# Holding three batches' tail loads behind a DMA transpose, in a linear-attention and feed-forward kernel

## The chip, the core and the metric

The kernel runs on one core of one Trainium2 chip. The metric is the device time of one execution in microseconds (us): 259.6 us is the median of three runs of the kernel before the change (259.32 to 260.02). A profile of one execution shows what each engine did: TensorE (PE in the profile, with its weight loads as PEld), VectorE (DVE), ScalarE (ACT), GpSimd (POOL) and SyncE (SP). SP and POOL are used here mostly to issue DMAs; SP's go by the hardware queue q1, POOL's by the software queue q0.

## What is computed

```python
def phi(x):
    return np.where(x > 0, x, np.exp(x) - 1.0) + 1.0
q_p, k_p = phi(q), phi(k)                      # q, k, v: (8, 8, 576, 64)
kv = np.einsum('bhsd,bhse->bhde', k_p, v)
z = np.sum(k_p, axis=2)
num = np.einsum('bhsd,bhde->bhse', q_p, kv)
den = np.einsum('bhsd,bhd->bhs', q_p, z)[..., None] + 1e-06
attn = num / den
x = attn.transpose(0, 2, 1, 3).reshape(8 * 576, 512)
a, b = x @ w1, x @ w2                          # (512, 1024) each
out = (a * b @ w3) @ w_out                     # (1024, 1024), (1024, 512)
```

All inputs and the output are float32; the kernel computes the matrix products in bfloat16.

## The kernel before

The 576 positions of each batch are split into 512 "main" positions (four rows of 128) and a tail of 64. Main positions are loaded in two halves of four heads each, 512 KB a load. The tails come as small DMAs of 64 KB: one for each half of the heads, so four for the q and k tails of a batch and two for its v tail. The 64-position tails of two batches share one row of 128, and all eight tails are collected into a ninth feed-forward block (c = 8). Since w3 and w_out are multiplied together once (wf), the feed-forward part is one product with w1, one with w2, an elementwise product and one product with wf.

All steps are emitted in one order, written out by hand as a list of short codes (ORDER, L520 to L546). Each engine executes its own instructions strictly in that order. A code is a letter, a batch (or block) and a part; a trailing "+" picks another engine for the step (for a load: POOL's queue in place of SP's; for a copy: VectorE in place of ScalarE). The codes that matter here:

- L, M, N: load of one half of k, q or v of a batch (load_qkv). R: tail load (load_tail), R4.0 for the q and k tails of batch 4, R4.1 for its v tail. The tail buffers are a ring of three for q and k and a ring of three for v, so the tails of one batch wait until those of an earlier batch have been used.
- x and X (exp on ScalarE), y and Y (max and add on VectorE), z and Z (min on VectorE): the three phi steps of k (small letters) and q (capitals). Part 2, as in x4.2, y4.2 and z4.2, is the step for both tails of the batch at once.
- v: copy of v into a bfloat16 tile; v4.2 is its tail.
- T: DMA transpose of phi(q) of a batch (qt_load, SP). It reads the whole tile qj, with the tails in it, and writes qt.
- K: kv and z of a batch (kv_full): 18 matmuls into a PSUM tile, then two copies. It needs k and v of the batch, with tails.
- A: num / den for one row of 128 positions (nat): four matmuls with qt as weights, then three VectorE instructions which leave xn. A4.4 and the like are the tail rows. K and A use the same PSUM tile, and there is only one such tile, so each waits until the one before has been read.
- D: DMA transpose of xn (xt_load, SP). F: one of the eight column blocks of the feed-forward product of a block (f_unit), eight matmuls in two PSUM banks, a copy on ScalarE and a product on VectorE; there are four such banks. O: 128 rows of output (o_unit), copied to o_sb. S: store of 256 rows (o_store, SP). There are two o_sb buffers, so the copy of an O step waits for the store of the second S step before.

SP executes its DMAs in the order of the list, so a transpose that waits for its input holds back all loads and stores behind it. Around the change the order on SP's queue is: T2.0, L3.0, N3.1, L3.1, L4.0, N3.0, S0.1, T3.0, D2.0, S0.0, L4.1, N4.1, M4.0, M4.1, M6.1, D3.0. On POOL's queue it is: R4.1 (two DMAs), R4.0 (four), R6.0 (four), R6.1 (two), R7.0 (four), R7.1 (two), and nothing behind these.

TensorE's order in the same place: A2.1, O0.0, ..., O1.1, O1.0, K3, O1.3, A3.0, O1.2, A3.2, F2.6, A3.3, F2.3, F2.1, A3.1, F2.0, F2.7, F2.4, F2.2, F2.5, A3.4, O2.3, F3.7, A2.4, F3.6.

GATES (L547) is a list of pairs "step<other": a load named there waits until the other step's DMA has completed. It acts in loaded (L551), which every load passes through; the wait is put on the last DMA of the load step. Before the change the list is empty.

Of the kernel before, what the change touches and what calls it, by code (L numbers as in the profile page):

```python
# [20 lines left out]
def kernel(  # L21
# [223 lines left out]

    def qt_load(b, part):
        t, s = qt_tile(b), ph["qt", b]
        i = NB if part else 0
        nc.sync.dma_start(out=t[:, i:NB + 2], in_=s[:, i * P:(NB + 2) * P], transpose=True)
# [271 lines left out]
    M0.0+ Y0.0 C1 E0 M0.1 I0 X0.0 E3 X0.1 L0.0 Y0.1 Z0.0 Z0.1 C0 y0.0 w0+ R0.0 R0.1 x0.0 E4 x0.2  # L521
    I1 w3+ L0.1+ x0.1 a0.0+ E1 y0.2 a0.1+ N0.1+ u0.2+ N0.0+ z0.0 R1.1 v0.1 y0.1 w4+ u3.2+ E2 w1+
    z0.2 z0.1 v0.0+ u4.2 E5 L1.0+ E7 v0.2+ E6 K0 M1.0+ M1.1+ w2 A0.3 y1.0 x1.0 L1.1+ u1.2 A0.0
    w5 R1.0+ u2.2+ w6 A0.2 B3.0 P0.3 Y1.0 z1.0 u5.2 I2 B3.1 X1.0 A0.1 w7+ P0.0 X1.1 Y1.1 N1.0+
    N1.1+ Z1.0 u6.2+ x1.2 P0.2+ x1.1 y1.2 P0.1 u7.2 Z1.1 y1.1 z1.1 B1.0 a1.0+ B1.1 v1.0+ B2.0
    B2.1 F0.6 B0.0 v1.1+ z1.2 T1.1 T0.1 v1.2 F0.7 M2.1 a1.1 K1+ F0.2 A1.2 F0.3 A1.3 F0.4 B0.1
    A1.0 P1.2 F0.5 P1.3 L2.1 A1.1 P1.0+ X2.1 R2.0+ h0 h1 A0.4 P1.1+ Y2.1 h2 h3 R3.0+ M3.1 i0
    A1.4 M2.0 i1 x2.1 X3.1 Z2.1 F1.7 F1.6 x2.2 L2.0 y2.1 y2.2 Y2.0 x3.2 R3.1+ X2.0 O0.3 N2.1
    x2.0 z2.1 N2.0 y2.0 z2.2 Z2.0 F1.0 M3.0 R5.0+ y3.2 T2.0 v2.1 L3.0 Y3.1 R2.1+ F1.5 N3.1 v2.0+
    z2.0 L3.1 Z3.1 v2.2+ O0.2 F1.2 F1.1 Y3.0 y5.2 z3.2 K2 F1.4 A2.2 X3.0 F1.3 L4.0 A2.3 x3.0  # L530
    O0.1 Z3.0 A2.0 x3.1 N3.0 y3.0 O0.0 v3.1 S0.1 A2.1 y3.1 R5.1+ z3.0 z3.1 v3.0 v3.2 O1.1+ O1.0
# [6 lines left out]
    L6.0 z6.2 O3.1 A5.2 L6.1 O3.0 A5.1 D1.1 Y6.1 Z6.1 F4.2 A5.0 Y6.0 F4.5 y6.1 F4.7 v6.0+ x6.1
    L7.0 x6.0 M7.0 A5.3 D3.1 x7.0 z6.1 F4.0 v6.1+ v6.2 F4.6 A4.4 Z6.0 F4.1 S3.0 F4.4 D5.0 A5.4
    y6.0 z6.0 F4.3 M7.1 F5.7 x7.2 y7.0 Y7.0 z7.2 L7.1 N7.0 K6+ z7.0 F5.6 F5.0 y7.1 X7.1 X7.0  # L540
    Z7.0 F5.5 S3.1 F5.3 Y7.1 T6.0 R7.1+ Z7.1 A6.3 T7.0 F5.1 O4.2 A6.1 x7.1 O4.1 A6.2 N7.1 z7.1
    F5.4 A6.0 F5.2 v7.1 v7.2+ O4.0 D6.0 D5.1 A6.4 v7.0 O4.3+ S4.1 K7 O5.0 F6.3 S4.0 O5.1 A7.4
    F6.5 F6.4 D7.1 F6.1 A7.3 O5.2 O5.3 A7.1 F6.2 F8.3 A7.0 F8.6 S5.1 F6.6 A7.2 S5.0 F6.0 F6.7
# [120 lines left out]
```

## Time and profile before

| | |
|---|---|
| median of three runs | 259.6 us |
| span of the profiled execution | 257.4 us |
| moved by DMA | 50.57 MB, mean 196 GB/s |
| share of the 16 DMA engines: SP's queue q1, POOL's queue q0 | 55.9%, 23.4% |
| full qt transposes, from issue to landing | 4.6 to 11.1 us |
| xt transposes, median from issue to landing | 4.4 us |

The profiled execution has its own time, the span; the runs' times lie about 2.2 us above it. "Busy" is the time in which an engine executes something, and an idle time is put down to what released the engine in the end. Times within the execution are microseconds from the start of its span. In a row of the timeline the first number is the start and the second the duration; "x2" says that two instructions are merged, and the bracket at the end is the idle time before with its releaser. A DMA's duration on SP or POOL is that of its issue, not of its transfer; "us to landing" runs from the issue to the completion.

### The profile page before, as it was taken

To read this page: it belongs to the slowest core of one execution; us is meant where nothing else is said; L and a number is where in the kernel's file an instruction comes from. 1 tells how busy PE (TensorE), PEld (TensorE's weight loads), DVE (VectorE), ACT (ScalarE), POOL (GpSimd) and SP (SyncE) were. 2 spreads that over 40 slices of the span, in tenths; PEclk is the share of its full clock that TensorE was granted. 3 is DMA by queue.
4 is the path that set the end of the run, shared out by engine and by line. 5 is a ranking of instruction groups with operands and counts; after the bars stand their busy time and mean duration, and the time that the engine had idled before them with its cause. 6 is when DMAs were issued, how large, how long until landed. Compare 5 with 4: busy or idle time off the path is not lost.

```text
span 257.4 us, 3788 instructions
## 1 busy us (share of the span) xinstructions
PE 232.3 (90%) x1352; PEld 117.8 (46%) x1368; DVE 159.1 (62%) x350; ACT 116.8 (45%) x180; POOL 49.1 (19%) x84
## 2 busy tenths in 40 slices
PE   0087899999999869999999999999999999999992
PEld 0063565554454434445445445454544444444540
DVE  0548589778899426897887899978235633343200
ACT  1404677357756506755562473645332312332221
POOL 8524479455045100600000000000000000000000
PEclk9999999999999979999999999999999999999999
DMA  6999999999989999799999998646512143001124
GB/s 220 211 237 289 311 255 245 200 248 283 299 247 291 194 242 347 182 284 222 356 308 211 289 263 272 154 89 151 200 20 91 74 83 163 3 0 30 42 115 139
DMA packets 63762, 50.57 MB, mean 196 GB/s; under 512 B 33536, under 2 KB 58368, under 8 KB 63744
## 3 DMA queue, kind: packets, MB, share of 16 engines
q1 hardware_dynamic: 54432, 37.10, 55.9%
q0 software_dynamic: 9152, 13.11, 23.4%
q8 instruction: 10, 0.16, 0.3%
q10 hardware_dynamic: 160, 0.13, 0.2%
q14 instruction: 8, 0.07, 0.1%
HBM read 38.80 MB, written 9.44 MB: 187 GB/s over the span
## 4 chain that ended last, share of the span: by engine, by line
PE 78%; DMA 13%; DVE 4%; issue 2%; ACT 0%; POOL 0%; DVEq 0%; ACTq 0%; POOLq 0%
PE a_ps L322 24%; PE b_ps L322 23%; PE o_ps L479 21%; DMA v<-in_v_dram 5%; DMA qt<-qj 4%; PE nd L280 4%; DMA wt_sb<-in_moe_w_out_dram 4%; PE kvp L225 2%; PE wf_ps L143 1%; PE kvp L229 1%; DVE y L173 1%; DVE vt L204 1%; PE o_ps L504 1%; DVE kj L198 1%; DVE qj L198 0%
## 5 line engine op out<-in xcount | busy, mean ns | idle before, releaser
L322 PEld LDWEIGHTS <-w_sb 128*128 128x128 bf16 x576 | 55.3, 98 | 61.8 <-issue 0.9
L328 DVE TENSOR_TENSOR ab<-a_sb,b_ps 128x512 bf16<-128x512 f32 x72 | 49.1, 685 | 38.2 <-PE b_ps L322 30.5
L322 PE MATMUL a_ps<-xt,w_sb 128*128 128x512 bf16 x256 | 67.3, 382 | 0.0
L322 PE MATMUL b_ps<-xt,w_sb 128*128 128x512 bf16 x256 | 66.7, 379 | 0.0
L327 ACT COPY a_sb<-a_ps 128x512 f32<-128x512 f32 x72 | 41.8, 585 | 54.4 <-PE a_ps L322 48.9
L479 PE MATMUL o_ps<-wf_sb,ab 128*128 128x512 bf16 x267 | 63.7, 383 | 0.8 <-issue 0.2
L479 PEld LDWEIGHTS <-ab 128*128 128x128 bf16 x280 | 27.0, 98 | 30.2 <-issue 0.8
L481 ACT COPY o_sb<-o_ps 128x512 f32<-128x512 f32 x29 | 16.8, 585 | 43.4 <-PE o_ps L479 27.2
L286 DVE TENSOR_TENSOR xn<-nd,r 128x512 bf16<-128x512 f32 x32 | 22.1, 691 | 1.1
L168 ACT ACTIVATE e<-q 128x1024 bf16<-128x1024 f32 x16 | 16.7, 1056 | 8.5 <-DMA q<-in_q_dram 8.5
L168 ACT ACTIVATE e<-k 128x1024 bf16<-128x1024 f32 x16 | 16.6, 1056 | 5.2 <-DMA k<-in_k_dram 5.0
L280 PE MATMUL nd<-kv,qt 128*128 128x130 bf16 (+1 forms) x160 | 16.1, 223 | 2.6 <-DMA qt<-qj 2.1
L136 PE MATMUL w3p<-ident,w3b 128*128 128x128 bf16 x64 | 5.7, 242 | 13.7 <-DMA w3b<-in_moe_w_dram 13.7
L280 PEld LDWEIGHTS <-qt 128*128 128x128 bf16 (+1 forms) x160 | 11.6, 101 | 14.0 <-issue 3.3
L284 DVE TENSOR_SCALAR r<-nd 128x8 f32<-128x8 f32 (+1 forms) x40 | 6.5, 162 | 16.8 <-PE nd L280 16.4
L173 DVE TENSOR_SCALAR y<-q 128x1024 bf16<-128x1024 f32 x16 | 11.2, 707 | 8.7 <-DMA q<-in_q_dram 8.7
L143 PE MATMUL wf_ps<-wt_sb,w3t 128*128 128x512 bf16 x61 | 14.9, 380 | 0.7 <-DMA wt_sb<-in_moe_w_out_dram 0.5
L104 POOL DMA_DIRECT2D qk32r<-in_q_dram x14 | 9.0, 648 | 19.1 <-ACT a_sb L327 16.5
L198 DVE TENSOR_TENSOR qj<-e,y 128x512 bf16<-128x512 bf16 x32 | 11.9, 417 | 0.4 <-ACT e L168 0.3
L198 DVE TENSOR_TENSOR kj<-e,y 128x512 bf16<-128x512 bf16 x32 | 11.9, 418 | 0.2
L225 PE MATMUL kvp<-vt,kj 128*128 128x130 bf16 x128 | 9.8, 219 | 2.4 <-DVE vt L204 1.8
L136 PEld LDWEIGHTS <-w3b 128*128 128x128 bf16 x64 | 4.6, 109 | 15.0 <-DMA w3b<-in_moe_w_dram 14.5
(54 smaller groups left out, 180.3 us busy)
## 6 DMA issues: line engine op xcount, KB each, us to landing
out_dram<-o_sb SPq DMA_DIRECT2D x16, 512.0 KB, 3.7
q<-in_q_dram SPq DMA_DIRECT2D x13, 512.0 KB, 8.0
k<-in_k_dram SPq DMA_DIRECT2D x13, 512.0 KB, 6.7
v<-in_v_dram SPq DMA_DIRECT2D x12, 512.0 KB, 8.0
w3b<-in_moe_w_dram POOLq DMA_DIRECT2D x8, 256.0 KB, 12.0
v<-in_v_dram POOLq DMA_DIRECT2D x4, 512.0 KB, 9.8
w_sb<-in_moe_w_dram POOLq DMA_DIRECT2D x8, 256.0 KB, 6.9
q<-in_q_dram POOLq DMA_DIRECT2D x3, 512.0 KB, 11.2
```

What stands on the lines that cost most here:

```text
L143: nc.tensor.matmul(wfs[i], w3ts[i][:, kc, :], wo_sb[:, kc, :], start=(kc == 0), stop=(kc == FC - 1))
L168: nc.scalar.activation(out=e, in_=x, func=AF.Exp)
L173: (nc.gpsimd if alt else nc.vector).tensor_scalar(out=y, in0=x, scalar1=0.0, scalar2=1.0, op0=ALU.max, op1=ALU.add)
L198: nc.vector.tensor_tensor(out=p[0][:, 2 * g + c].rearrange("p j u d -> p u j d"), in0=e[:, c], in1=y[:, c], op=ALU.min)
L225: nc.tensor.matmul(kvp[:, i, g * W:(g + 1) * W], kj[:, hp, j].rearrange("p u d -> p (u d)"), vt[:, j, 2 * hp:2 * hp + 2, :].rearrange("p h ...
L280: nc.tensor.matmul(nd[rows, g, i * 2 * E1:(i + 1) * 2 * E1], w, kvs[b % 2][:, i, g].rearrange("p u e -> p (u e)"), start=True, stop=True)
L286: nc.vector.tensor_tensor(out=dst.rearrange("p (g h) e -> p g h e", g=2), in0=v4[:, :, :, 0:D], in1=r[rows].unsqueeze(3).to_broadcast([n, ...
L322: nc.tensor.matmul(ps, w[:, kc, f * P:(f + 1) * P], xt_of(c)[:, :, kc, :], start=(kc == 0), stop=(kc == KC - 1))
L327: nc.scalar.copy(out=a_sb, in_=a_ps)
L328: nc.vector.tensor_mul(out=abs_[c][:, f, :], in0=a_sb, in1=b_ps)
L479: nc.tensor.matmul(o_ps, ab[:, f, m * P:(m + 1) * P], wf_sb[:, f, :], start=(f == 0), stop=(f == FC - 1))
L481: copy_of(alt)(out=rows_of(c, m // 2)[:, m % 2], in_=o_ps)
```

## The change

One list of steps is replaced by another, one gate is added, and the T step records its DMA so that a gate can name it. The computation stays the same. In the list:

- L4.0 moves from a place ahead of A2.3 to one behind S0.0; on SP's queue it thereby goes from ahead of N3.0, S0.1, T3.0, D2.0 and S0.0 to behind them.
- v4.2+ moves from behind L4.1 to behind Z4.1.
- y4.2 and x4.2 move from around F2.7 to behind X4.0, and z4.2 from behind Z4.0 to ahead of it.
- The gate R4.1<T3.0 makes the second of R4.1's two DMAs on POOL's queue wait for the completion of T3.0. What stands behind it in that queue (R4.0, R6.0, R6.1, R7.0, R7.1) can't be issued earlier either.

Cut to the lines that differ in content:

```diff
-        nc.sync.dma_start(out=t[:, i:NB + 2], in_=s[:, i * P:(NB + 2) * P], transpose=True)
+        return nc.sync.dma_start(out=t[:, i:NB + 2], in_=s[:, i * P:(NB + 2) * P], transpose=True)
...
-    Y3.0 y5.2 z3.2 K2 F1.4 A2.2 X3.0 F1.3 L4.0 A2.3 x3.0
+    Y3.0 y5.2 z3.2 K2 F1.4 A2.2 X3.0 F1.3 A2.3 x3.0
...
-    T3.0 D2.0 S0.0 K3 R4.1+ R4.0+ O1.3 A3.0 O1.2 A3.2 L4.1 v4.2+ F2.6 A3.3 F2.3 N4.1 y4.1 F2.1
-    M4.0 x4.1 A3.1 x4.0 F2.0 M4.1 y4.2 M6.1 v5.2+ x4.2 F2.7 Y4.0 D3.0 F2.4 z4.1 X4.1 F2.2 Y4.1
-    v4.1 S1.0 F2.5 Z4.1 M5.0 N4.0 X4.0 Z4.0 A3.4 z4.2 y4.0 O2.3 F3.7 M5.1 Y5.0 v4.0 A2.4 F3.6
+    T3.0 D2.0 S0.0 L4.0 K3 R4.1+ R4.0+ O1.3 A3.0 O1.2 A3.2 L4.1 F2.6 A3.3 F2.3 N4.1 y4.1 F2.1
+    M4.0 x4.1 A3.1 x4.0 F2.0 M4.1 M6.1 v5.2+ F2.7 Y4.0 D3.0 F2.4 z4.1 X4.1 F2.2 Y4.1
+    v4.1 S1.0 F2.5 Z4.1 v4.2+ M5.0 N4.0 X4.0 y4.2 x4.2 z4.2 Z4.0 A3.4 y4.0 O2.3 F3.7 M5.1 Y5.0 v4.0 A2.4 F3.6
...
-    GATES = ""
+    GATES = "R4.1<T3.0"
...
         elif t == "T":
-            qt_load(b, i)
+            held[s] = qt_load(b, i)
```

More of the change, by code (lines that the diff above doesn't have):

```diff
@@ L520 @@
     ORDER = """
[L521 to L531, printed above, removed]
@@ L532 @@
-    T3.0 D2.0 S0.0 K3 R4.1+ R4.0+ O1.3 A3.0 O1.2 A3.2 L4.1 v4.2+ F2.6 A3.3 F2.3 N4.1 y4.1 F2.1
-    M4.0 x4.1 A3.1 x4.0 F2.0 M4.1 y4.2 M6.1 v5.2+ x4.2 F2.7 Y4.0 D3.0 F2.4 z4.1 X4.1 F2.2 Y4.1
-    v4.1 S1.0 F2.5 Z4.1 M5.0 N4.0 X4.0 Z4.0 A3.4 z4.2 y4.0 O2.3 F3.7 M5.1 Y5.0 v4.0 A2.4 F3.6
-    z4.0 L5.0 T4.0 R6.0+ x5.2 Y5.1 X5.0 F3.1 N5.1 Z5.0 S1.1 O2.2+ K4 F3.2 M6.0 x6.2 X5.1 A4.2
-    Z5.1 F3.4 z5.2 F3.5 y5.0 A4.1 F3.0 L5.1 F3.3 N5.0 y5.1 X6.1 y6.2 O2.1 A4.3 R6.1+ N6.0 S2.1
-    x5.1 N6.1 v5.0+ T5.0 O2.0 x5.0 v5.1+ A4.0 R7.0+ z5.1 D4.0 z5.0 X6.0 O3.3 y7.2 O3.2+ K5+ S2.0
@@ L538 @@
[L538 to L543, printed above, removed]
@@ L544 @@
-    D7.0 O6.3+ O6.2 O6.1 O6.0+ F7.1 F7.7 F7.2 F8.0 S6.1 F8.7 S6.0 F8.1 F8.5 F7.4 F8.2 F8.4 F7.6
-    O8.2 F7.5 H8.2 F7.3 F7.0 Q8.3 O7.0 O7.1 O7.2 S7.0 O7.3 O8.0 S7.1 O8.1 S8.0
+    M0.0+ Y0.0 C1 E0 M0.1 I0 X0.0 E3 X0.1 L0.0 Y0.1 Z0.0 Z0.1 C0 y0.0 w0+ R0.0 R0.1 x0.0 E4 x0.2 I1
+    w3+ L0.1+ x0.1 a0.0+ E1 y0.2 a0.1+ N0.1+ u0.2+ N0.0+ z0.0 R1.1 v0.1 y0.1 w4+ u3.2+ E2 w1+ z0.2
+    z0.1 v0.0+ u4.2 E5 L1.0+ E7 v0.2+ E6 K0 M1.0+ M1.1+ w2 A0.3 y1.0 x1.0 L1.1+ u1.2 A0.0 w5 R1.0+
+    u2.2+ w6 A0.2 B3.0 P0.3 Y1.0 z1.0 u5.2 I2 B3.1 X1.0 A0.1 w7+ P0.0 X1.1 Y1.1 N1.0+ N1.1+ Z1.0
@@ new lines @@
+    u6.2+ x1.2 P0.2+ x1.1 y1.2 P0.1 u7.2 Z1.1 y1.1 z1.1 B1.0 a1.0+ B1.1 v1.0+ B2.0 B2.1 F0.6 B0.0
+    v1.1+ z1.2 T1.1 T0.1 v1.2 F0.7 M2.1 a1.1 K1+ F0.2 A1.2 F0.3 A1.3 F0.4 B0.1 A1.0 P1.2 F0.5 P1.3
+    L2.1 A1.1 P1.0+ X2.1 R2.0+ h0 h1 A0.4 P1.1+ Y2.1 h2 h3 R3.0+ M3.1 i0 A1.4 M2.0 i1 x2.1 X3.1 Z2.1
+    F1.7 F1.6 x2.2 L2.0 y2.1 y2.2 Y2.0 x3.2 R3.1+ X2.0 O0.3 N2.1 x2.0 z2.1 N2.0 y2.0 z2.2 Z2.0 F1.0
+    M3.0 R5.0+ y3.2 T2.0 v2.1 L3.0 Y3.1 R2.1+ F1.5 N3.1 v2.0+ z2.0 L3.1 Z3.1 v2.2+ O0.2 F1.2 F1.1
@@ new lines @@
+    Y3.0 y5.2 z3.2 K2 F1.4 A2.2 X3.0 F1.3 A2.3 x3.0 O0.1 Z3.0 A2.0 x3.1 N3.0 y3.0 O0.0 v3.1 S0.1
+    A2.1 y3.1 R5.1+ z3.0 z3.1 v3.0 v3.2 O1.1+ O1.0 T3.0 D2.0 S0.0 L4.0 K3 R4.1+ R4.0+ O1.3 A3.0 O1.2
+    A3.2 L4.1 F2.6 A3.3 F2.3 N4.1 y4.1 F2.1 M4.0 x4.1 A3.1 x4.0 F2.0 M4.1 M6.1 v5.2+ F2.7 Y4.0 D3.0
+    F2.4 z4.1 X4.1 F2.2 Y4.1 v4.1 S1.0 F2.5 Z4.1 v4.2+ M5.0 N4.0 X4.0 y4.2 x4.2 z4.2 Z4.0 A3.4 y4.0
+    O2.3 F3.7 M5.1 Y5.0 v4.0 A2.4 F3.6 z4.0 L5.0 T4.0 R6.0+ x5.2 Y5.1 X5.0 F3.1 N5.1 Z5.0 S1.1 O2.2+
@@ new lines @@
+    K4 F3.2 M6.0 x6.2 X5.1 A4.2 Z5.1 F3.4 z5.2 F3.5 y5.0 A4.1 F3.0 L5.1 F3.3 N5.0 y5.1 X6.1 y6.2
+    O2.1 A4.3 R6.1+ N6.0 S2.1 x5.1 N6.1 v5.0+ T5.0 O2.0 x5.0 v5.1+ A4.0 R7.0+ z5.1 D4.0 z5.0 X6.0
+    O3.3 y7.2 O3.2+ K5+ S2.0 L6.0 z6.2 O3.1 A5.2 L6.1 O3.0 A5.1 D1.1 Y6.1 Z6.1 F4.2 A5.0 Y6.0 F4.5
+    y6.1 F4.7 v6.0+ x6.1 L7.0 x6.0 M7.0 A5.3 D3.1 x7.0 z6.1 F4.0 v6.1+ v6.2 F4.6 A4.4 Z6.0 F4.1 S3.0
+    F4.4 D5.0 A5.4 y6.0 z6.0 F4.3 M7.1 F5.7 x7.2 y7.0 Y7.0 z7.2 L7.1 N7.0 K6+ z7.0 F5.6 F5.0 y7.1
+    X7.1 X7.0 Z7.0 F5.5 S3.1 F5.3 Y7.1 T6.0 R7.1+ Z7.1 A6.3 T7.0 F5.1 O4.2 A6.1 x7.1 O4.1 A6.2 N7.1
@@ L546 @@
+    z7.1 F5.4 A6.0 F5.2 v7.1 v7.2+ O4.0 D6.0 D5.1 A6.4 v7.0 O4.3+ S4.1 K7 O5.0 F6.3 S4.0 O5.1 A7.4
+    F6.5 F6.4 D7.1 F6.1 A7.3 O5.2 O5.3 A7.1 F6.2 F8.3 A7.0 F8.6 S5.1 F6.6 A7.2 S5.0 F6.0 F6.7 D7.0
+    O6.3+ O6.2 O6.1 O6.0+ F7.1 F7.7 F7.2 F8.0 S6.1 F8.7 S6.0 F8.1 F8.5 F7.4 F8.2 F8.4 F7.6 O8.2 F7.5
+    H8.2 F7.3 F7.0 Q8.3 O7.0 O7.1 O7.2 S7.0 O7.3 O8.0 S7.1 O8.1 S8.0
     """
-    GATES = ""
+    GATES = "R4.1<T3.0"
     ctx.enter_context(tc.manual_schedule())
```

## The prediction

> **What bounds the kernel now.** I read the share of the engines and the 40 slices first, then the waits, then the timeline round the one hole that they show, then the DMA traffic in that hole.
>
> ```profile
> PE 232.3 (90%) x1352; PEld 117.8 (46%) x1368; DVE 159.1 (62%) x350; ACT 116.8 (45%) x180; POOL 49.1 (19%) x84
> PE   0087899999999869999999999999999999999992
> PEclk9999999999999979999999999999999999999999
> DMA  6999999999989999799999998646512143001124
> ```
> A slice is 6.4 us. TensorE is the bound from slice 8 on, but for slices 13 and 14 (84 to 97 us): there it is 80% and then 60% busy, and the only dip of its granted clock before the end lies there. The DMA engines are nearly full until 160 us, so traffic that is moved stays somewhere.
>
> ```profile
> PE nd L280 <- DMA qt<-qj: 2.1, 1, 2.1
> PE kvp L225 <- ACT vt L204: 0.6, 1, 0.6
> ACT vt L204 <- DMA v<-in_v_dram: 5.8, 4, 1.9
> ACT o_sb L481 <- DMA out_dram<-o_sb: 16.2, 3, 8.5
> ```
> The waits that cost TensorE time after 60 us: 2.1 us for a transposed q (step A3.0 waits for T3.0), and 0.6 us for a cast of v (K3 waits for v3.0, which waits for load N3.0).
>
> ```profile
> 90.20:92.20 2.00, 0.00 (x0) 0.00 (x0) 0.00 (x0) 0.00 (x0) 0.00 (x0) 1.00 1.18 192
> 92.20:93.20 1.00, 0.97 (x8) 0.62 (x9) 0.47 (x3) 0.00 (x0) 0.00 (x0) 1.00 1.49 134
> 93.20:96.60 3.40, 3.40 (x13) 1.47 (x12) 1.33 (x4) 0.00 (x0) 0.00 (x0) 0.50 1.08 304
> 96.60:100.00 3.40, 3.40 (x21) 1.60 (x19) 1.50 (x5) 2.05 (x4) 0.00 (x0) 0.99 1.10 345
> ```
> Busy time by stretch (PE, PEld, DVE, ACT, POOL), then granted clock, DMA share and GB/s. All engines stand still from 90.2 to 92.2 while DMA is full; one microsecond after TensorE starts again its clock is halved for 3.4 us, which costs 3.4 x (1 - 0.50) = 1.7 us.
>
> ```profile
> 74.22 1.23 POOL L104 DMA_DIRECT2D v32r<-in_v_dram  x2 [12.16 <-DVE vr L210]
> 75.09 1.25 SPq L489 DMA_DIRECT2D out_dram<-o_sb  x1
> 77.94 1.23 POOL L104 DMA_DIRECT2D qk32r<-in_q_dram  x2
> 81.07 5.93 SPq L249 DMA_TRANSPOSE qt<-qj  x1
> 82.02 0.77 POOL L104 DMA_DIRECT2D qk32r<-in_k_dram  x1 [0.65 <-DMA v32r<-in_v_dram]
> 87.09 3.89 SPq L311 DMA_TRANSPOSE xt<-xn  x1
> 91.07 0.62 SPq L489 DMA_DIRECT2D out_dram<-o_sb  x1
> ```
> Start, duration, engine. T3.0 goes out at 81.07 and lands 11.1 us later, at 92.17; D2.0 (87.09, lands after 8.3) and store S0.0 (91.07, after 6.6) queue behind it. Ahead of T3.0 on SP's queue stand five loads (L3.0, N3.1, L3.1, L4.0, N3.0, issued 72.1 to 75.0) and store S0.1. Beside them POOL issues R4.1, R4.0 and R6.0 from 74.22 to 82.8.
>
> ```profile
> DMA packets 1451, 1.45 MB, mean 362 GB/s; under 512 B 39, under 2 KB 1451, under 8 KB 1451
> q1 hardware_dynamic: 1451, 1.45, 105.1%
> DMA packets 1001, 1.17 MB, mean 259 GB/s; under 512 B 108, under 2 KB 919, under 8 KB 1001
> q1 hardware_dynamic: 828, 0.83, 79.2%
> q0 software_dynamic: 173, 0.34, 30.5%
> ```
> DMA in 74.5 to 78.5 us (two lines) and in 79.0 to 83.5 us (three). SP's queue (q1) moves 1.45 / 4.0 = 0.363 MB per us alone, and 0.83 / 4.5 = 0.184 beside the tails (q0).
>
> **The change, part by part.** No arithmetic is added or removed; every piece is a shift.
>
> *Ahead of T3.0.* L4.0 (0.524 MB) leaves the queue: 0.524 / 0.363 = 1.4 us. The second half of R4.1 and all of R4.0 and R6.0 (9 DMAs of 64 KB, 0.59 MB) wait: in 79.0 to 83.5 the tails cost q1 4.5 x (0.363 - 0.184) = 0.8 MB, or 2.2 us. The same q1 traffic then ends thus: L3.1 landed at 79.6 (73.3 + 6.3), before the first tail did (80.4), N3.0 now comes 1.4 us later, S0.1 another 1.4: about 82.5, not 87.2. So T3.0 meets an almost empty queue. Its own time is not shown for that place; the nearest rows bound it: 4.6 us (T7.0, the shortest of the full qt transposes) and 7.4 (T4.0, issued behind a full queue). It lands at 85.7 to 88.5; I take 86.5, nearer the free one.
>
> *What TensorE then does.* N3.0 lands near 81.1 instead of 85.7 (74.4 + 11.3), so ACT's second cast starts at 84.1, behind the first, instead of 85.73. K3 starts when O1.0 ends at 86.2 (kj is ready at 85.86): 0.6 us won. It lasts 1.4 us (86.83 to 88.24), O1.3 1.7 us: A3.0 can start at 89.3, against 92.23. Even the late bound 88.5 is hidden by K3 and O1.3. Without the hole of 2.1 us I expect no clock dip: 1.7 us. Together 0.6 + 2.1 + 1.7 = 4.4 us; bounds 2.7 (dip stays) and 4.7 (small gaps close too). [...] The stretch 93.2 to 96.6 comes right behind the hole, so I go by the row.
>
> *The next in line.* F2.6 (95.56 before, 91.5 then) needs D2.0. D2.0 now waits for A2.1's xn (83.91), moves behind T3.0's data and lands at 88.5 to 91.3: 4.4 us (D3.0, undisturbed) behind 84.1, or 8.3 less 1 behind 84.0. Hidden, by 0.2 us at the late end. S0.0 goes out near 87 instead of 91.07 and lands 3.7 us (median of the stores) to 6.6 us later, at 90.7 to 93.6; ACT's copies of O1.3 and O1.2 wait for it, and F2.1 (95.4) wants the bank that ACT's next copy frees, so 93.7 is the last good time. Hidden too, narrowly at the late end.
>
> *POOL.* Behind the gated DMA stand R4.0, R6.0, R6.1, R7.0 and R7.1 and nothing else. They start at about 86.5 and their data meets S0.0, L4.0, L4.1 and N4.1. [...] L4.1 is wanted by y4.1 at 101.55 - 4.4 = 97.1. Queue: D2.0 done 88.5, S0.0 1.4, then 1.05 MB at 0.184 = 5.7, landing 0.8: 96.4. I cost it at nothing, at most 0.5. L4.0 lands before it and is used after it.
>
> *The moved phi steps.* v4.2 (0.63 us of DVE from its start to the next), y4.2 (0.34) and z4.2 (0.34) now stand ahead of Z4.0 and A3.4 on DVE. Before, DVE waits 0.36 to 0.44 us for TensorE ahead of each of the products at 107.18, 108.91 and 110.64, so taking them away from earlier places wins nothing. A3.4's xnr ends at 113.82 before, 1.3 later now, and A2.4 on TensorE, at 114.36 with no wait, shares its PSUM tile: 113.82 + 1.31 - 114.36 = 0.8 us lost (bounds 0 and 1.3). x4.2 moves behind X4.0 on ACT, which has idle time there (1.5 us before 112.74). T4.0 is issued at the same place, as its last input ends at about 114.0 against 114.28. R7.0 must now wait for y4.2.
>
> Sum: -4.4 + 0.8 = -3.6 us. Span 257.4 to 253.8. The profiled span stands 2.2 us below the median of 259.6, so the time is 259.6 - 3.6 = 256.0 us. From 97 us on TensorE has no wait over 0.2 us, so nothing later swallows the gain.
>
> **Rivals.**
> (1) The dip has another cause and stays: 259.6 - 2.7 + 0.8 = 257.7. For it: TensorE is busy again for a whole microsecond before the clock falls. [...] Against: it is the one dip before the end, behind the one hole of that size since 60 us.
> (2) T4.0 takes T3.0's place. Before, it lands at 121.75 and A4.2 runs at 122.75: slack 1.0. R7's six tails now start about 3 us later in the program and may fall beside T4.0 as R6.0's did beside T3.0. If T4.0 too takes 11.1 from 114.0 - 4.4 = 109.6, it lands at 120.7, A4.2 wants it at 122.75 - 3.6 = 119.1: 1.6, and 1.7 if the clock falls: 256.0 + 3.3 = 259.3. Half of that, or a late L4.1, gives 257 to 258. Against: only 0.4 MB of tails, and one load less than ahead of T3.0.
> (3) Slower: the released tails hold S0.0 at its old landing, 97.7. Then ACT frees F2.6's bank at 97.7 + 1.07 + 0.6 = 99.4, and F2.1 waits from 95.4: 4.0, with a new dip 5.7: 256.0 + 5.7 = 261.7. It decides from a landing of 93.7, and is slower than before from 95.6 on with the dip. For it: S0.0 stands behind two transposes and beside nine tails. Against: SP is free for it 4 us sooner.
> (4) The change does not do it: T3.0 stays slow although the queue is empty (T5.0 took 11.1 with no tails beside it). Then A3.0 waits as before and only A2.4's 0.8 is new: 260.4. Against: T5.0 had eight DMAs ahead of it.
>
> **How the numbers follow.** Forecast 0.66 (255.2 to 256.8 by the terms' own bounds); rival 1 0.08; partial 2 at 257 to 258 0.09, full 2 0.05; rival 3 0.08; rival 4 0.04. A measurement of this kernel (259.32 to 260.02) tells about 0.3%, 0.8 us, from no change. Faster: 0.66 + 0.08 + 0.09, less a little for the edges, 0.82. Same: full 2 and edges, 0.07. Slower: 3, most of 4: 0.11. The range runs from 255.0 to 258.2, over forecast, rival 1 and partial 2, which leaves out about 0.2.
>
> **What would show it.** T3.0 lands 5 to 7 us after its issue; no TensorE wait at A3.0 and K3; granted clock 1.00 from 88 to 96; S0.0 landed before 93.7; a wait of A2.4's nd on DVE of about 0.8 us near 110. Wrong if TensorE shows a new wait over 1 us at F2.6, F2.1 or A4.2, or a second dip.

## The result, and the profile after

The changed kernel is slower: a median of 262.73 us against 259.38 (nine runs of each), ratio 1.0092 with a 95% interval of 1.0064 to 1.012. The profiled execution's span is 260.7 us against 257.4. The forecast was 256.0, with a range from 255.0 to 258.2. (Here and below the ratio is worked out over the undisturbed executions alone, the medians are of all, and the one isn't the quotient of the others.)

The share of the engines and the 40 slices of the changed kernel:

```profile
PE 233.0 (89%) x1352; PEld 117.7 (45%) x1368; DVE 159.3 (61%) x350; ACT 117.0 (45%) x180; POOL 49.3 (19%) x84
PE   0087999999999999785999999999999999999992
PEclk9999999999999999999799999999999999999999
DMA  6999999999999999999999989826701343000225
```

The weak slices 13 and 14 of before (84 to 97 us) are full now, and so is the clock there. New weak slices stand at 16 to 18 (104 to 124 us), and a dip of the clock right behind them. The stall at T3.0 is gone, and a longer one stands some 30 us later. The waits of the changed kernel from 60 to 130 us name it (total us, times, longest):

```profile
ACT e L168 <- DMA q<-in_q_dram: 4.1, 2, 2.3
PE nd L280 <- DMA qt<-qj: 3.9, 1, 3.9
PE nd L280 <- DVE xnr L286: 0.7, 1, 0.7
PE o_ps L479 <- DVE ab L328: 0.6, 1, 0.6
PE a_ps L322 <- DMA xt<-xn: 0.6, 1, 0.6
```

To see where time was won and lost, follow the same instructions in both traces. TensorE's timeline has, of the kernel before, the first matmuls of A3.4, A2.4, A4.2 and A4.1 (start, duration):

```profile
110.46 0.41 PE L280 MATMUL nd<-kv,qt 128*64 128x130 bf16 x4
114.36 0.41 PE L280 MATMUL nd<-kv,qt 128*64 128x130 bf16 x4
122.75 0.39 PE L280 MATMUL nd<-kv,qt 128*128 128x130 bf16 x4
126.43 0.39 PE L280 MATMUL nd<-kv,qt 128*128 128x130 bf16 x4
```

and of the changed kernel A3.4, O2.3, F3.7, A2.4 and A4.2, with the wait in front of each:

```profile
105.62 0.41 PE L280 MATMUL nd<-kv,qt 128*64 128x130 bf16 x4
...
108.00 0.82 PE L479 MATMUL o_ps<-wf_sb,ab 128*128 128x512 bf16 x3 [0.61 <-DVE ab L328]
...
109.40 1.04 PE L322 MATMUL a_ps<-xt,w_sb 128*128 128x512 bf16 x4 [0.57 <-DMA xt<-xn]
...
112.02 0.41 PE L280 MATMUL nd<-kv,qt 128*64 128x130 bf16 x4 [0.72 <-DVE xnr L286]
...
124.47 0.61 PE L280 MATMUL nd<-kv,qt 128*128 128x130 bf16 x4 [3.89 <-DMA qt<-qj]
```

At A3.4 the changed kernel leads by 110.46 - 105.62 = 4.84 us. At A2.4 the lead is 114.36 - 112.02 = 2.34: three waits (0.61, 0.57, 0.72) and small gaps took 2.5. At A4.2 it is 122.75 - 124.47 = -1.72: another 4.06 lost, of which 3.89 is one wait for T4.0, the DMA transpose of batch 4's q. A4.1 starts at 129.73 against 126.43, so 1.58 more went by there; from then on the changed kernel is 3.30 behind to the end. The windows show what that last piece is (PE, PEld, DVE, ACT, POOL, then granted clock, DMA share, GB/s):

```profile
122.00:124.30 2.30, 0.00 (x0) 0.00 (x0) 0.00 (x0) 0.00 (x0) 0.00 (x0) 1.00 1.12 223
124.30:127.70 3.40, 3.23 (x11) 1.47 (x12) 1.73 (x5) 0.59 (x1) 0.00 (x0) 0.50 1.07 336
127.70:131.00 3.30, 3.30 (x19) 1.60 (x18) 2.02 (x4) 0.59 (x1) 0.00 (x0) 1.00 1.10 356
```

The same pattern as before the change, at another transpose: all engines still, DMA full, then a clock of 0.50 for 3.4 us. The timeline of SP's and POOL's queues of the changed kernel shows what stood beside the transposes (start, duration of the issue):

```profile
81.26 2.82 SPq L249 DMA_TRANSPOSE qt<-qj  x1
84.17 3.16 SPq L311 DMA_TRANSPOSE xt<-xn  x1
88.25 0.62 POOL L104 DMA_DIRECT2D v32r<-in_v_dram  x1 [13.21 <-DMA qt<-qj]
...
99.05 6.36 SPq L311 DMA_TRANSPOSE xt<-xn  x1
110.15 1.23 POOL L104 DMA_DIRECT2D qk32r<-in_q_dram  x2 [12.01 <-DVE qj L193]
...
110.86 6.88 SPq L249 DMA_TRANSPOSE qt<-qj  x1
112.83 1.33 POOL L104 DMA_DIRECT2D v32r<-in_v_dram  x2
```

T3.0 (81.26) lands 6.4 us later and D2.0 (84.17) 6.0 us later, against 11.1 and 8.3 before. The held tail goes out at 88.25, R4.0 and R6.0 follow to 94.8, R6.1 at 96.52: beside M4.0, M4.1 and D3.0. R7.0 goes out from 110.15, because it reuses the tail tile that batch 4's moved phi steps read last, and R7.1 at 112.83: six tails around T4.0 (110.86). T4.0 lands after 13.6 us where it took 7.4 before, when R7.0 had gone out at 105.53; D3.0 lands after 10.3 where it took 4.4. Time to landing is told in two parts below: the wait for the first packet (4.7 of T3.0's 11.1 us before the change, when N3.0 had landed; 3.9 of T4.0's 13.6 here), and the time in which the packets move (8.1 of those 13.6). The experiments need both.

### The profile page after: what moved, and what is told of

Its sections match the earlier page's. It is cut to its first block, busy times and chain, and to the rows that moved or that the text cites. A ratio compares the mean times of both kernels' runs of the same rounds, so it can differ in the third digit from the quotient of the medians.

```text
span 260.7 us, 3791 instructions
## 1 busy us (share of the span) xinstructions
PE 233.0 (89%) x1352; PEld 117.7 (45%) x1368; DVE 159.3 (61%) x350; ACT 117.0 (45%) x180; POOL 49.3 (19%) x84
## 4 chain that ended last, share of the span: by engine, by line
PE 60%; DMA 25%; DVE 7%; issue 3%; ACT 2%; SPq 1%; POOL 0%; DVEq 0%; ACTq 0%; POOLq 0%
PE o_ps L479 18%; PE b_ps L322 17%; PE a_ps L322 17%; DMA v<-in_v_dram 11%; DMA qt<-qj 5%; DMA q<-in_q_dram 5%; DMA wt_sb<-in_moe_w_out_dram 3%; PE nd L280 3%; PE kvp L225 2%; PE wf_ps L143 1%; DVE qj L198 1%; DVE kj L198 1%; SPq L95 1%; DVE y L173 1%; PE kvp L229 1%
## 5 line engine op out<-in xcount | busy, mean ns | idle before, releaser
L479 PE MATMUL o_ps<-wf_sb,ab 128*128 128x512 bf16 x267 | 63.0, 379 | 1.4 <-DVE ab L328 0.6
L104 POOL DMA_DIRECT2D v32r<-in_v_dram x12 | 7.9, 659 | 27.3 <-DMA qt<-qj 13.2
L173 DVE TENSOR_SCALAR y<-k 128x1024 bf16<-128x1024 f32 x16 | 11.0, 686 | 0.5 <-DMA k<-in_k_dram 0.3
## 6 DMA issues: line engine op xcount, KB each, us to landing
w3b<-in_moe_w_dram POOLq DMA_DIRECT2D x8, 256.0 KB, 12.0
w_sb<-in_moe_w_dram POOLq DMA_DIRECT2D x8, 256.0 KB, 7.1
```

The costliest lines, as they stand in the source:

```text
L104: ins = (nc.gpsimd if alt else nc.sync).dma_start(out=t[g * R:(g + 1) * R, i].rearrange("p (h d) -> p h d", d=D), in_=src[name][b, g * 4:( ...
L173: (nc.gpsimd if alt else nc.vector).tensor_scalar(out=y, in0=x, scalar1=0.0, scalar2=1.0, op0=ALU.max, op1=ALU.add)
L479: nc.tensor.matmul(o_ps, ab[:, f, m * P:(m + 1) * P], wf_sb[:, f, :], start=(f == 0), stop=(f == FC - 1))
```

## The experiments

Two theories stood against each other at the start. A: the tail loads cost a transpose that they fly beside more than they cost anything else, so the loss is T4.0 with R7 beside it. B: the loss comes from the queue as a whole, L4.0 and the tails moved into a later and equally full stretch, whatever they meet. All ratios are against the kernel before, with 95% intervals.

**r7_held.** R7.0's first DMA waits for T4.0, and everything else is as in the changed kernel. For that the tail load of batch 7 returns its first DMA instead of its last.

```diff
+        first = None
...
+                first = first or ins
-        return ins
+        return first if b == 7 else ins
...
-    GATES = "R4.1<T3.0"
+    GATES = "R4.1<T3.0 R7.0<T4.0"
```

> The changed kernel with a second gate: the first DMA of batch 7's q and k tails (R7.0) waits until T4.0 has landed, and R7.1 behind it. Theory A (tails beside a transpose slow its small packets): T4.0 has no tails beside it and lands in 6 to 8.5 us instead of 13.6, A4.2's wait of 3.9 us and the clock dip behind it (1.6) go, the time is 262.7 - 5.5 = 257.2 us, and it is faster than before by 1.5 to 2.5 us. Theory B (T4.0 is late through SP's own loads ahead of it): T4.0 still needs over 11 us, the time stays within 1 us of 262.7. Both: the losses of about 2 us ahead of A2.4 stay.

Measured: 257.34 us, ratio 0.9898 (0.9854 to 0.9942). T4.0 goes out at 109.69 and lands after 7.5 us; A4.2 doesn't wait and starts at 119.24, and no clock dip follows. One gate on R7 takes 5.4 us off the changed kernel's median (5.0 by the two ratios) and turns its loss into a gain. The waits left on TensorE are small: 0.8 (xnr), 0.5 (D3.0, landing after 9.1) and 0.3 us. The two packet counts below belong to the stretches in which T4.0's packets move, most of those under 512 bytes. First the changed kernel, 114.5 to 122.7 us, then r7_held, 113.0 to 116.7 us:

```profile
DMA packets 2771, 1.20 MB, mean 147 GB/s; under 512 B 2425, under 2 KB 2686, under 8 KB 2771
q1 hardware_dynamic: 2597, 0.85, 101.2%
q0 software_dynamic: 174, 0.35, 27.6%
```

```profile
DMA packets 2628, 0.87 MB, mean 236 GB/s; under 512 B 2350, under 2 KB 2628, under 8 KB 2628
q1 hardware_dynamic: 2628, 0.87, 127.3%
```

About the same packets of SP's queue (q1) take 8.2 us beside 0.35 MB of tails and 3.7 us without. Those 0.35 MB, at the 236 GB/s of the stretch without tails, would be 1.5 us; the stretch grew by 4.5.

**r61_held.** The same gate earlier: R6.1's second DMA, and so R7 behind it, waits for T4.0.

```diff
-    GATES = "R4.1<T3.0"
+    GATES = "R4.1<T3.0 R6.1<T4.0"
```

> As the kernel with R7 held, but the second gate sits on batch 6's v tail (R6.1), so one more DMA is kept out of the stretch 96 to 105 us as well. Theory A: T4.0 lands in 6 to 8.5 us, and M4.1 lands 0.3 to 0.5 us earlier than in the changed kernel, so the time is that with R7 held or up to 0.4 us less. Theory B: within 1 us of 262.7.

Measured: 257.74 us, 0.9911 (0.9878 to 0.9944); T4.0 lands after 7.6, D3.0 after 8.8, and TensorE waits 1.1 us for xnr (A2.4) and 0.6 for F2.5's product (O2.3). Not to be told from r7_held: what counts is that R7 is kept from T4.0, not where the gate stands.

**half_tails.** The gate on the last of R7.0's four DMAs, so that three tails fly beside T4.0 in place of six or none.

```diff
-    GATES = "R4.1<T3.0"
+    GATES = "R4.1<T3.0 R7.0<T4.0"
```

> The changed kernel with a gate on the last of R7.0's four DMAs: three of batch 7's six tail DMAs go at about 110 us, beside T4.0, the other three wait for T4.0's landing. Theory A predicts a dose: T4.0 lands between the 7.5 us that it took with none beside it and the 13.6 us with six, at 9.5 to 12; A4.2 waits 0.5 to 2.5 us; time 258 to 261. Theory B' (it is enough that any tail is beside it, or only the last ones matter): 13 us or 7.5 us, and the time of the changed kernel or that with R7 held.

Measured: 257.58 us, 0.9916 (0.9886 to 0.9946). The time expected was missed, because T4.0 lands after 9.3 us, a little under the 9.5 to 12 expected, and that is still in time for A4.2. In these three runs the landing follows the dose: 7.5 us with no tail beside it, 9.3 with three, 13.6 with six. The number of tails alone doesn't fix it, as no_gate and phi_only will show; how many of their bytes move among T4.0's packets orders the runs better (last section).

**no_gate.** The changed order without the gate.

```diff
-    GATES = "R4.1<T3.0"
+    GATES = ""
```

> The changed kernel without its gate: L4.0 and the phi steps of batch 4's tails stay moved. Theory A: R7's tails still have to wait for y4.2 and z4.2, which stand late, so they still fall beside T4.0: T4.0 over 10 us and A4.2 waits over 2 us; ahead of T3.0 only L4.0 is gone (1.4 us), A3.0 waits about 0.7 us; the time is 260 to 263. Rival (the gate alone is the harm): T4.0 lands in under 9 us and the time is at most 258.5.

Measured: 258.41 us, 0.9914 (0.9876 to 0.9952), below the 260 to 263 expected. In the profiled execution, which took 259.89, T3.0 needs 9.8 us and A3.0 waits 1.89 for it; T4.0 needs 10.3, with R7's six tails out from 112.07 to 116, and A4.2 waits 0.66, not over 2. TensorE reaches A4.2 later here, so the late T4.0 costs less. The gate, added to the rest of the change, turns a gain into a loss.

**phi_back.** Gate and L4.0's place stay; v4.2, x4.2, y4.2 and z4.2 return to where they stood before, which frees R7's buffer earlier.

```diff
-    A3.2 L4.1 F2.6 ... M4.1 M6.1 v5.2+ F2.7 ... Z4.1 v4.2+ M5.0 N4.0 X4.0 y4.2 x4.2 z4.2 Z4.0 A3.4 y4.0
+    A3.2 L4.1 v4.2+ F2.6 ... M4.1 y4.2 M6.1 v5.2+ x4.2 F2.7 ... Z4.1 M5.0 N4.0 X4.0 Z4.0 A3.4 z4.2 y4.0
```

> The changed kernel with v4.2, x4.2, y4.2 and z4.2 back at their places of before; the gate and L4.0's place stay. Theory A: R7's tails are issued near 100 us as soon as y4.2 has run, and are through before T4.0's packets: T4.0 lands in under 9 us, no wait at A4.2; A2.4's wait for the shared PSUM tile (0.7 us) goes; DVE waits up to 2 us at v4.2 for the late tail of v, near 92 to 94 us; D3.0 lands later by 0.5 to 1.5 us. Time 257 to 260. Rival C (the loss comes from the traffic pushed into 92 to 104 us whatever the phi steps do): 261 to 264, with A4.2 still waiting.

Measured: 261.54 us, 1.0053 (1.0018 to 1.0088): a miss. Its timeline shows why:

```profile
99.36 6.12 SPq L311 DMA_TRANSPOSE xt<-xn  x1
101.08 1.23 POOL L104 DMA_DIRECT2D qk32r<-in_q_dram  x2 [3.24 <-DVE vr L210]
...
103.58 1.23 POOL L104 DMA_DIRECT2D v32r<-in_v_dram  x2
...
113.67 1.89 PE L322 MATMUL a_ps<-xt,w_sb 128*128 128x512 bf16 x4 [4.75 <-DMA xt<-xn]
```

R7 does go out nine microseconds earlier, and so it meets D3.0 (99.36) in place of T4.0. D3.0's packets move from 103.1 to 111.2, in 8.0 us beside 0.29 MB of tails; in the kernel before the change they took 2.7. D3.0 lands after 14.3 us, F3.7 waits 4.75 us for it, and the clock is down for 6.8 us behind that. A2.4's wait is gone, as expected. The victim changed, the mechanism stayed. (The profiled execution is the slowest of its twelve, with 263.1 us, so the median holds less than these waits.)

**load_only.** The kernel before with L4.0 behind S0.0, nothing else.

```diff
-    ... X3.0 F1.3 L4.0 A2.3 ... T3.0 D2.0 S0.0 K3
+    ... X3.0 F1.3 A2.3 ... T3.0 D2.0 S0.0 L4.0 K3
```

> Kernel before, only L4.0 moved behind S0.0. Tails still go beside T3.0, which has one load less ahead of it: it lands after about 9.8 us (as in the run without the gate) instead of 11.1, A3.0 waits 1 to 2 us. R7's tails are released at their old place in the program, about 105 us. Theory A: T4.0 as before, 7 to 9 us, no wait at A4.2 over 1 us; 256.5 to 259.5, depending on whether the clock dips.

Measured: 258.1 us (254.86 to 261.13), 0.9869 (0.9814 to 0.9923). T3.0 needs 9.5 us, so A3.0 waits 1.56, and no dip follows in the profiled execution; D3.0 needs 5.7 and T4.0 8.0.

**gate_only.** The kernel before with the gate, nothing else.

```diff
-    GATES = ""
+    GATES = "R4.1<T3.0"
```

> Kernel before, only the gate. T3.0 lands after 6.5 to 8 us, A3.0 and K3 do not wait. v4.2 waits on DVE for the late v tail near 92 to 94 us. Theory A: R7's tails are issued near 101 to 104 us and fall beside D3.0 as in the run with the phi steps put back: D3.0 over 9 us, F3.7 waits 1 to 5 us; time 258 to 262. If instead the harm needs L4.0 in the late stretch as well: D3.0 under 7 us and 256 to 257.5.

Measured: 257.89 us, 0.9913 (0.9878 to 0.9948). T3.0 needs 7.3 us. R7 (100.51 to 104.4) is out beside D3.0 here too (99.06, 10.5 us): F3.7 waits 2.17 and a dip follows. That R7 did this isn't shown: D3.0's packets move from 102.3 to 105.8, in 3.6 us, and D3.0 lands only 3.7 us after the last of them. The time is just below the 258 to 262 expected: it gains, since A3.0's wait is gone.

**phi_only.** The kernel before with only the phi steps moved.

```diff
-    A3.2 L4.1 v4.2+ F2.6 ... M4.1 y4.2 M6.1 v5.2+ x4.2 F2.7 ... Z4.1 M5.0 N4.0 X4.0 Z4.0 A3.4 z4.2 y4.0
+    A3.2 L4.1 F2.6 ... M4.1 M6.1 v5.2+ F2.7 ... Z4.1 v4.2+ M5.0 N4.0 X4.0 y4.2 x4.2 z4.2 Z4.0 A3.4 y4.0
```

> Kernel before, only v4.2, x4.2, y4.2 and z4.2 moved. T3.0 lands after 11 us and A3.0 waits 2 us as before, with the clock dip in some executions; A2.4 waits 0.7 to 1 us for xnr. Theory A: R7's tails are issued near 114 us and fall beside T4.0: over 10 us, A4.2 waits 0.5 to 3 us. Time 260 to 264. If the late phi steps cost only A2.4's wait: 260.2.

Measured: 260.72 us, 1.0039 (1.0007 to 1.0071). T3.0 stays slow (12.2 us). The hole in front of the dip is 2.27 us at O1.3 here, whose bank waits for a copy that a store holds up, and A3.0 follows at once. A2.4 waits 0.96; R7, later here (114.84 to 118.9), leaves T4.0 at 9.2 us and A4.2 without a wait, where over 10 us and a wait had been expected. By themselves the moved steps cost about one A2.4 wait.

**gate_phi.** Gate and moved phi steps, with L4.0 at its old, early place.

```diff
-    ... X3.0 F1.3 A2.3 ... T3.0 D2.0 S0.0 L4.0 K3
+    ... X3.0 F1.3 L4.0 A2.3 ... T3.0 D2.0 S0.0 K3
```

> The gate and the moved phi steps, with L4.0 at its place of before: the last cell of the three parts. T3.0 lands after about 7 us; the stretch 88 to 104 us has one load less than in the changed kernel, so M4.1 and D3.0 come about 1.5 us earlier. Theory A: R7's tails still meet T4.0: 9 to 13 us, A4.2 waits 0.5 to 3 us. Time 258.5 to 261.5, between the gate alone (257.9) and all three (262.7).

Measured: 259.63 us, 1.0007 (0.997 to 1.0044). T3.0 needs 6.7 us even with L4.0 ahead of it, so the gate alone frees T3.0. In the profiled execution, the slowest of its ten with 262.57 us, T4.0 still needs 13.0 and A4.2 waits 3.38 before a dip; the median holds less of that.

The parts of the change, alone and together (medians in us and ratios; beside them the kernel before runs at 259.3 to 259.9):

| | phi steps at the old place | phi steps moved |
|---|---|---|
| neither | 259.4; 1 | 260.7; 1.004 (phi_only) |
| L4.0 later | 258.1; 0.987 (load_only) | 258.4; 0.991 (no_gate) |
| gate | 257.9; 0.991 (gate_only) | 259.6; 1.001 (gate_phi) |
| both | 261.5; 1.005 (phi_back) | 262.7; 1.009 (the change) |

They don't add up. With the phi steps at the old place, L4.0's move and the gate each gain, and together they lose; with the phi steps moved, the move gains, the gate comes out at the kernel before, and together they lose. Both push traffic into the stretch where D3.0, or T4.0, goes out.

**r60_later.** Is D3.0's part of the loss the tails' too? R6.0's first DMA waits for D3.0 here, so no tail but R4's can meet D3.0.

```diff
-        return ins
+        return first if (b, part) in ((6, 0),) else ins
...
-    GATES = "R4.1<T3.0"
+    GATES = "R4.1<T3.0 R6.0<D3.0"
...
         elif t == "D":
-            xt_load(b, i)
+            held[s] = xt_load(b, i)
```

> The changed kernel with R6.0 and all tails behind it on POOL's queue held until D3.0 has landed; R7 is not held behind T4.0. It parts the two losses. If the 2 us ahead of A2.4 come from tails in 92 to 105 us: M4.1 lands 2 to 3 us earlier than in the changed kernel, D3.0 after 4.4 to 7 us instead of 10.3, only A2.4's 0.7 us of wait for xnr stays there. Theory A: R6.0, R6.1 and R7 (12 DMAs) then meet T4.0, which takes 11 us or more, and A4.2 waits 1 to 4 us. Time 258 to 262. If T4.0 lands in under 9 us nonetheless, theory A falls.

Measured: 263.54 us, 1.0148 (1.0109 to 1.0188). D3.0 needs 6.0 us and the waits at O2.3 and F3.7 are gone; only A2.4's stays (1.06). But R6 and R7 now stand beside T4.0 together: it needs 14.3 us, A4.2 waits 4.62, and a dip of 6.8 us follows. Both parts of the mechanism came out as expected, and the time is somewhat worse than expected. It tells the two losses apart: two of the waits before A2.4 (O2.3 and F3.7) come from the released tails R6, the wait at A4.2 from the tails beside T4.0.

The two losses differ in kind. D3.0's packets in the changed kernel (104.3 to 107.0 us), and in the kernel before (105.05 to 107.75):

```profile
DMA packets 2186, 0.69 MB, mean 254 GB/s; under 512 B 2094, under 2 KB 2168, under 8 KB 2185
q1 hardware_dynamic: 2185, 0.67, 123.7%
DMA packets 2078, 0.52 MB, mean 194 GB/s; under 512 B 2078, under 2 KB 2078, under 8 KB 2078
q1 hardware_dynamic: 2078, 0.52, 104.2%
```

No tail (q0) moves among them, and they take 2.7 us in both. D3.0 is late because its first packet comes 5.3 us after its issue, behind M4.1 (landed at 104.2), where it was 1.2 before; and it lands 2.4 us after its last packet, where it was 0.5. The second also happens in r7_held (2.4), and no run shows why. So the waits at O2.3 and F3.7 are closer to theory B: the tails make loads late (M4.1 landed after 13.5 us where it took 8.8), and a transpose is queued behind these. The loss at T4.0 is what theory A says.

**each_own and each_own_early_load.** A first try to give every transpose its free stretch: R4 behind T3.0, R6.0 behind D3.0, R6.1 behind T4.0, R7 behind T5.0; phi steps at the old place, but v4.2 behind M4.1. The second has L4.0 early.

```diff
-        return ins
+        return first if (b, part) in ((6, 0), (6, 1), (7, 0)) else ins
...
-    F2.0 M4.1 M6.1 v5.2+ F2.7 ... Z4.1 v4.2+ M5.0 N4.0 X4.0 y4.2 x4.2 z4.2 Z4.0 A3.4 y4.0
+    F2.0 M4.1 v4.2+ y4.2 M6.1 v5.2+ x4.2 F2.7 ... Z4.1 M5.0 N4.0 X4.0 Z4.0 A3.4 z4.2 y4.0
...
-    GATES = "R4.1<T3.0"
+    GATES = "R4.1<T3.0 R6.0<D3.0 R6.1<T4.0 R7.0<T5.0"
```

> Each batch of tails behind a transpose of its own: R4 behind T3.0, R6.0 behind D3.0, R6.1 behind T4.0, R7 behind T5.0; L4.0 behind S0.0; x4.2, y4.2 and z4.2 at their places of before, v4.2 behind M4.1. Theory A: no transpose of a main block on the way has more than a few tails beside it: T3.0 6 to 7.5, D3.0 4.4 to 7, T4.0 7 to 9 us; A3.0, F3.7, A2.4 and A4.2 wait under 0.5 us each. Time 254 to 256.5, faster than both kernels and than that with R7 held (257.3). Rival: the tails only move the same waits on (x6.2, T5.0, x7.2): 257 or more.

> As the kernel with each tail behind its own transpose, but L4.0 at its place of before. T3.0 lands 1 to 1.5 us later, still hidden by K3 and O1.3; L4.1 to M6.1 and D3.0 land about 1.5 us earlier. If the stretch 88 to 104 us binds: 0.3 to 1 us faster than with L4.0 moved; if not, equal within 0.5 us.

Measured: 268.37 us, 1.033 (1.0292 to 1.0369), and 268.42, 1.0331 (1.0293 to 1.0368): both a miss, through a mistake in the design. TensorE's waits are below 0.4 us up to 135 us in the first. Then, in its timeline:

```profile
135.49 1.22 POOL L105 DMA_DIRECT2D qk32r<-in_q_dram  x2 [15.02 <-DMA qt<-qj]
...
144.82 0.43 DVE L175 TENSOR_SCALAR yr<-qk32r 128x512 bf16<-128x512 f32 x1 [11.87 <-DMA qk32r<-in_k_dram]
...
146.77 0.59 PE L282 MATMUL nd<-kv,qt 128*128 128x130 bf16 x4 [10.29 <-DVE kv L236]
```

R7, held for T5.0, goes out at 135.49, and y7.2 wanted it 11.87 us before it came. The order on VectorE puts y7.2 ahead of work that K5 and the next A step need, so TensorE stood for 10.29 us, and the clock was down for 10.2 behind that. A gate has a last good time as well.

**own_and_free and own_early_load.** The same without the gate on T5.0: R7 follows R6.1, behind T4.0. own_early_load has L4.0 at its place of before.

```diff
-    GATES = "R4.1<T3.0"
+    GATES = "R4.1<T3.0 R6.0<D3.0 R6.1<T4.0"
```

> As the kernel with each tail behind its own transpose, but R7 is no longer held behind T5.0 (there y7.2 waited 11.9 us for it on DVE and K6 with it); it follows R6.1, behind T4.0. Theory A: no TensorE wait over 0.6 us between 72 and 200 us; A4.2 runs 4 us earlier than before; 255 to 256.5 us. If the tails that now meet T5.0 cost there what they cost at T4.0: T5.0 over 13 us, a wait at A5.2, 258 or more.

> The same with L4.0 at its place of before. Up to K5 its like ran 0.9 us ahead of the kernel with L4.0 moved and 4.95 ahead of the kernel before: 254 to 255.5 us, and 0.5 to 1 us under the other. If L4.0's place does not matter any more: equal within 0.4 us.

Measured: own_and_free 257.73 us, 0.9921 (0.9889 to 0.9952), above the 255 to 256.5 expected, with one wait of 1.19 us for xn; own_early_load 256.09 us (254.91 to 257.68), 0.9874 (0.9838 to 0.9909), span 254.5, also a little above its 254 to 255.5. In the latter T3.0 needs 7.2 us, D2.0 5.0, D3.0 5.8, T4.0 7.8, and no tail moves among the packets of any of them. T5.0 goes out with eight tails in flight and takes 13.1, of which 8.8 go by before its first packet; it took 11.1 before the change with no tail in flight. TensorE waits for it nowhere. Its slices, and its waits of TensorE from 72 us on:

```profile
PE   0087999999989999999989999999999999999992
PEclk9999999999999999999999999999999999999999
```

```profile
PE nd L282 <- DVE xn L288: 0.7, 1, 0.7
PE a_ps L324 <- DMA xt<-xn: 0.2, 1, 0.2
```

From 72 us on no wait above 0.74 us and no dip is left. It has the lowest median of all that was run, but the intervals of the other faster versions overlap with its own, so the order among them is not settled.

**plain_beside.** Is it the tails that hurt, or any traffic of POOL's queue? r7_held, with load L5.0 (512 KB) moved to POOL's queue beside T4.0, behind R6.

```diff
-    O2.3 F3.7 M5.1 Y5.0 v4.0 A2.4 F3.6 z4.0 L5.0 T4.0 R6.0+ x5.2 ... A4.3 R6.1+ N6.0
+    O2.3 F3.7 M5.1 Y5.0 v4.0 A2.4 F3.6 z4.0 R6.0+ R6.1+ L5.0+ T4.0 x5.2 ... A4.3 N6.0
...
-    GATES = "R4.1<T3.0"
+    GATES = "R4.1<T3.0 L5.0<D3.0 R7.0<T4.0"
```

> The kernel with R7 held behind T4.0, but a plain load of 512 KB (L5.0) is taken from SP's queue and issued from POOL, held there until D3.0 has landed, so that it runs beside T4.0 where R7's tails ran in the changed kernel. It tells whether tails as such slow a transpose or any traffic of POOL's queue. If any traffic: T4.0's packets need 5 us or more from first to last (3.3 with nothing beside them), landing after 9 to 13 us, 258 to 262 us. If tails as such (64 KB DMAs, or their 256-byte pieces): 4 us or less, landing after 6 to 8 us, within 1 us of 257.3.

Measured: 257.3 us, 0.9913 (0.9878 to 0.9948); T4.0 needs 7.3 us, and its packets move from 114.2 to 117.8, in 3.6 us:

```profile
q1 hardware_dynamic: 2352, 0.61, 109.7%
q0 software_dynamic: 83, 0.27, 21.9%
```

0.27 MB of POOL's queue moved beside the transpose without slowing it (3.7 us in r7_held). But these packets lie in the first 1.5 us of the stretch alone, so the run speaks for the small tail loads as the cause rather than for any load of POOL's queue, and doesn't settle it.

## Why the prediction was wrong

Point by point, by its own steps:

- *T3.0, K3, A3.0.* Right. T3.0 landed 6.4 us after its issue, at 87.70 (forecast 86.5, bounds 85.7 to 88.5). K3 and A3.0 no longer wait, A3.0 starts at 89.08 (forecast 89.3), the clock is full, and the lead at A3.4 is 4.84 us (forecast 4.4, bounds 2.7 to 4.7). The mechanism was right too: T3.0's first packet comes 1.2 us after its issue, where it came 4.7 after it before, when N3.0 had landed. gate_phi and gate_only show that the gate does most of this: T3.0 takes 6.7 and 7.3 us with L4.0 still ahead of it, and 9.5 and 9.8 with L4.0 moved and no gate, against 11.1.
- *D2.0 and S0.0 behind it.* Right: they landed at 90.2 and 92.3, inside 88.5 to 91.3 and 90.7 to 93.6, and TensorE waited for neither.
- *The moved phi steps.* Right in what was priced: A2.4 waited 0.72 us (forecast 0.8, bounds 0 to 1.3).
- *The POOL step failed first.* That the released tails would meet S0.0, L4.0, L4.1 and N4.1 was right, and then this was costed "at nothing, at most 0.5", because only L4.1 was looked at. The sentence that closes the sum, "nothing later swallows the gain", rested on TensorE having no wait from 97 us on, and no wait is not the same as time to spare. L4.1 was indeed in time; what came late were M4.1 (landing 13.5 us after its issue in place of 8.8, at 104.2, so that X4.1's exp waited 2.3 us and the copy and product of F2.5 behind it came late) and D3.0 (10.3 us in place of 4.4, queued behind M4.1). Before, X4.1 ran at 106.73, 3.8 us after M4.1 had landed; a TensorE that is 4.8 us ahead uses that up by itself, so the gain of the first part had made the next transfers urgent. O2.3 (0.61) and F3.7 (0.57) paid for it; the lead shrank by 2.5 us to A2.4, of which 0.7 had been foreseen. r60_later ties the two waits to R6: with R6 behind D3.0 both are gone. R6.1 had been left out of the sum as well.
- *The T4.0 step failed worst.* The forecast saw that "R7.0 must now wait for y4.2" and gave it no price; T4.0 was taken to go as before. In fact R7's release went to 110.15, on top of T4.0: 4.6 us later by the clock while TensorE was 2 to 5 us ahead, so some 7 to 9 us later in the program and not the "about 3" of the rival. It cost 3.89 us of waiting and 1.58 more in the stretch with the dip, together 5.5 us. r7_held shows it directly: with R7 behind T4.0 the wait and the dip are gone, and the median is 5.4 us lower. The rival in which T4.0 takes T3.0's place had the right mechanism, with a chance of 0.14 in its two forms; it was given 11.1 us of landing where 13.6 came, and so 259.3 us.
- *The size was off by less.* The price of the tails was taken from what they do to loads (0.363 to 0.184 MB per us on SP's queue). The DMA stretch from 92.0 to 104.2 us of the changed kernel, with eleven tail DMAs in it, has:

```profile
q1 hardware_dynamic: 2643, 2.62, 86.0%
q0 software_dynamic: 352, 0.72, 23.3%
```

  and the nearest stretch of the kernel before, 94.2 to 103.7 us, almost none:

```profile
q1 hardware_dynamic: 2813, 3.14, 106.4%
q0 software_dynamic: 16, 0.00, 0.1%
```

  2.62 / 12.2 = 0.215 against 3.14 / 9.5 = 0.331 MB per us: SP's queue lost 12.2 x (0.331 - 0.215) = 1.4 MB beside 0.72 MB of tails, 2.0 to 1. The price that was used is 0.8 MB for 0.34, 2.4 to 1. At T4.0 it was 4.5 x 0.236 = 1.06 MB for 0.35, 3.0 to 1. So a transpose paid somewhat more than loads, but the old price would already have given 3.5 of the 4.5 us; what the sum lacked was that R7 meets T4.0, and that D3.0 stands behind the loads that pay. T3.0's 11.1 us of before was no price for that meeting: 4.7 of them went by before its first packet.
- *The clock term was mis-sized for the median.* 1.7 us belongs to the profiled execution. Of 52 executions of the kernel before, timed beside the r7_held and half_tails sets, only 13 have a mean granted clock of 0.993 or less (a rough sign of a dip in the middle); their median is 260.55 us against 259.53 for the others. So the median never held the 1.7 us whole. Where the new waits are taken away, own_early_load comes out at 256.09, some 3.3 us below the kernel before, where the sum of the first part said 4.4.

Still open is why a transpose's packets, and loads too, lose two to three times the bytes of the tails beside them, and whether any other small load would do the same.

## What to carry to other kernels

A gate moves work: list every transfer that stands behind it, with the last use of each, and look up which transposes will be in flight when they go out; price them there, and price also what queues behind the loads that they slow (here D3.0, 10.3 us to landing against 4.4, behind M4.1). A stage that becomes faster wants its next inputs sooner, so transfers that had time to spare may have none (M4.1 had 3.8 us, and the lead was 4.84). A buffer ring ties a load to the last reader of an old tile, so moving that reader also moves a load that the list of the change doesn't name (R7.0, from 105.53 to 110.15). And a stall that one profiled execution shows, such as a halved clock, is worth in the median what it costs times how often it comes (1.7 us, with its sign in 13 of 52 executions).
